# An attention and Fourier kernel: eight banks and later loads in the Projection, Fourier tiles split later, and another order in the prologue's last block

## The chip, the cores and the metric

The kernel runs on one NeuronCore of a Trainium2 chip. The metric is device microseconds from one launch, smaller is better. The core has five engines that work side by side, each through its own instructions in order: TensorE (PE, matmuls; its weight loads are shown as PEld), VectorE (DVE), ScalarE (ACT), GpSimd (POOL) and SyncE (SP), which here gives out most of the DMA transfers. GpSimd gives out some too. TensorE writes only to PSUM, which has eight banks; VectorE and ScalarE empty them.

## The reference

Two layers of attention, each followed by a Fourier mixing layer, on one sequence of 2048 tokens with 640 features and 32 heads of 20:

```python
def _A_ref(x, wqkv, wo):
    ...
    q, k, v = qkv[0], qkv[1], qkv[2]
    scores = jnp.einsum("bhqd,bhkd->bhqk", q, k) * (Dh ** -0.5)
    p = _softmax(scores, axis=-1)
    o = jnp.einsum("bhqk,bhkd->bhqd", p, v)
    return (lambda x, *d: x.transpose(*d))(o, 0, 2, 1, 3).reshape(B, S, D) @ wo

def _B_ref(x, dft_seq_re, dft_seq_im, dft_hid_re, dft_hid_im):
    a = jnp.einsum("bsd,ed->bse", x, dft_hid_re)
    b = jnp.einsum("bsd,ed->bse", x, dft_hid_im)
    y = jnp.einsum("ts,bse->bte", dft_seq_re, a) - jnp.einsum("ts,bse->bte", dft_seq_im, b)
    return y

x = A_x
x = x + _A_ref(_layernorm(x, axis=-1), A_wqkv, A_wo)
x = x + _B_ref(_layernorm(x, axis=-1), ...)
x = x + _A_ref(_layernorm(x, axis=-1), A_wqkv, A_wo)
x = x + _B_ref(_layernorm(x, axis=-1), ...)
```

## The kernel before

**Arithmetic.** Operands are split into a high and a low part (`split`, L85: one copy that rounds, one subtraction), and most products are made of three matmuls, high by high, high by low and low by high (`three`, L93, and `passes`, L100). One layer runs through four stages.

**Prologue** (`Qkv.prologue`, L293). The rows are normalized and transposed in four blocks of 512 tokens. For each block `tb` a product of 15 matmuls (L103) is made for the first chunk of q (k = 0 in the loop) and one for the first chunk of k (k = 1). `keep` (L198) empties each: ScalarE writes the rounded part and the squares (L218), for k VectorE takes the maximum of the squares over the blocks (L220), VectorE writes the low part (L221), and GpSimd gives out the store of both (L222). `norms` (L225) sums the squares over the features of a head with one matmul (L230) and takes their maximum (L231). Then come the values of four token tiles (`own`, L336), 15 matmuls each, which ScalarE empties (L263). Behind the last block's norms the code writes out, in this order: `bound` (L456), which makes from the norms' maxima the shift that goes into the exponent and stores it (L465); `qshift` (L519), four loads of shift rows into the q tiles (L522), for which the store must have landed; and `kload` (L492), eight loads of the second half of k. These stand ahead of the values of that block in the code; the values need none of them. The attention's first scores need the shift rows.

**Attention** (`Attention.sweep`, L571). 512 steps of scores (L536), exponentials on ScalarE (L539) and value sums (L547), with the remaining products of q, k and v in between. Each finished block of queries is emptied and divided by VectorE (`finish`, L552) and written to the tensor o by GpSimd's DMAs (L568). The last of these belong to the last quarter of the tokens.

**Projection** (`Project.run`, L1087). Eight stages p of two token tiles n = 2p, 2p + 1. `product(n)` (L1013) multiplies the tile of o by wo, in two halves of 15 matmuls, each into a bank of its own; for n up to 4 three of the five feature chunks were done during the attention (`begin`, L998), and 12 matmuls a product remain. VectorE adds the product to the residual rows (L1021). `moments(p)` (L1030) stores the sum (L1033), squares it on ScalarE (L1039), makes mean and scale on GpSimd, and folds mirrored columns on VectorE (L1050, L1051). `normal(k)` (L1070) normalizes and folds the rows of stage k some stages later; four of these folds end in the operands `xn` of the Fourier stage. Three kinds of transfers go through SP's queue in the order of the code: `load(p + 3)` (L1008, L1011) brings residual rows into one of four tiles, the one that stage p - 1 used; `fetch` (L983, L990) brings o for two pairs of stages at a time, in stages 1 and 3, four calls of two transfers each, into the tiles that the products just made have left; and the store of `moments`. In stage 1 three tiles of Fourier coefficients are loaded as well (L1209).

**Fourier** (`Fourier.run`, L1340). 16 sums, each of nine matmuls, go over the coefficient tiles in `ORDER`; `accumulate` (L1224) adds tile m into three banks, b0 to b2 or b3 to b5. After the last tile of four, `turn` (L1237) copies and splits the three banks. `parts(i)` (L1211) splits the raw coefficient tile of position i: one ScalarE copy (L1217), one VectorE subtraction (L1219), into one of six buffers, so that position i takes the buffer of position i - 6. Positions 0 to 5 are split during the Projection, the others in this loop. `middle` (L1242) works out one single row in four steps between the sums; its third step is twelve small matmuls (L1267, pturn) on a row that VectorE has made (L1257, L1259, L1262). `hidden` (L1297) makes the second transform, eight times.

What the code says ahead of the change, in the places that it touches:

```python
p = bank(f"b{4 + (2 * n + i) % 4}", [128, 512], "py")[:, :HD]     # Project.product
...
if p:                                                             # Project.run
    s.load(p + 3)
for n in (2 * p, 2 * p + 1):
    s.product(n)
...
s.parts(i + s.AHEAD)                                              # Fourier.run, AHEAD = 6
```

The order in each queue is that of the code: nothing is reordered between the instructions of one engine.

Of the kernel before, what the change touches and what calls it, by code (L numbers as in the profile page):

```python
# [19 lines left out]
ND = D // 128  # L20
NT = S // 128
NB = S // 512
# [3 lines left out]
NQ = NT // 4  # L26
# [6 lines left out]
HD = D // 2  # L33
# [6 lines left out]
def mha_fnet_kernel(ctx, tc, x_in, wqk, wv, wo, seq, hid, nat_seq, nat_hid, out):  # L40
# [33 lines left out]
    def bank(tag, shape, name):  # L74
        return pools["pool"].tile(list(shape), F32, name=name, tag=tag)
# [60 lines left out]
    class Qkv:  # L136
# [58 lines left out]
        def product(s, p, w, tb, dc):  # L195
            return passes(p, (w[:, 0, dc], w[:, 1, dc]), s.xt[tb, dc], dc)
# [96 lines left out]
        def prologue(s, vals, xt, fill, att):  # L293
            s.xtp, s.fill, room = xt, fill, s.room
            if s.given:
                for k in (2, 3):
                    s.load(k)
            s.top = const.tile([128, 2, ND, NB], F32, name="top", bufs=2)
            V.memset(s.top, 0.0)

            def values():
                s.wv = fill("wv", [ND, 2, HD], F32R, "wv")
                for dc in range(ND):
                    split(s.wv[:, dc, 0], s.wv[:, dc, 1], s.wvraw[dc])

            if s.given:
                s.turn(0)
                values()
            else:
                s.stats(0)  # L310

                s.fetch(0, att.kq, "k3", wait=True)
                s.fetch(ND, att.kq, "k4")
                for k in (2, 3):
                    s.load(k)
                s.load_values()
                s.norm(0)
                s.stats(1)
                s.early(0)
                s.norm(1)  # L320
                s.early(1)
                s.turn(0, wait=True)
                values()

            def ones(t):
                s.v[t] = vals(f"v{t}", [H * VW + 12], F32, "v")
                G.memset(s.v[t][:, :H * VW].rearrange("p (a c) -> p a c", c=VW)[:, :, DH:], 1.0)
                G.memset(s.v[t][:, H * VW:], 1.0)

            for t in range(NT - ND):  # L330
                ones(t)
            def later(tb, k, f):
                if tb + 2 < NB:
                    f(2 * tb + 4 + k)

            def own(tb, n):  # L336
                t = 4 * tb + n
                p = s.bank([128, HD], "pv")
                for dc in range(ND):
                    for f in s.value(p, t, dc):  # L340
                        f()
                s.own(p, t, 0, False)

            for tb in range(NB):

                sq, late = [], tb == 0
                if late:
                    for k in range(2):
                        later(tb, k, s.load)
                for k in range(2):  # L350
                    p = s.bank([128, 512], "pqk")
                    for dc in range(ND):
                        for f in s.product(p, s.w[k], tb, dc):
                            f()
                    sq.append(s.keep(p, k * ND, tb, False, (room, fill)[k]))
                    if late:
                        s.stats(2 + k)
                        continue
                    later(tb, k, s.stats)
                if late:  # L360
                    for n in range(4):
                        own(tb, n)
                        if n < 2:
                            s.norm(2 + n)
                            later(tb, n, s.stats)
                if tb == 0:
                    att.setup()
                elif tb == 1:
                    for t in range(NT - ND, NT):
                        ones(t)  # L370
                if tb + 1 < NB:
                    s.turn(tb + 1)
                    for k in range(2):
                        later(tb + 1, k, s.load)
                for k in range(2):
                    later(tb, k, s.norm)
                    s.norms(s.bank, k * ND, tb, sq[k])
                if tb == 0:
                    att.qload(0, 0, None)
                elif tb == 1:  # L380
                    s.fetch(ND + 1)
                    for j in range(2):
                        att.kload(0, 0, j)
                elif tb == 2:
                    s.w1 = s.weights(s.fill("w", [2, ND, 128], F32R, "wqk"), ND + 1, True)
                    s.fetch(1)
                    att.zeros(room)
                elif tb == NB - 1:
                    list(s.bound(0, room))
                    att.qshift(0, 0)  # L390
                    for j in range(2):
                        att.kload(0, 1, j)
                if not late:
                    for n in range(4):
                        own(tb, n)
            s.made |= {0, ND}


# [559 lines left out]
    class Project:  # L958
# [54 lines left out]
        def product(s, n):  # L1013
            x = s.x[n // 2][:, n % 2]
            for i in range(2):
                p = bank(f"b{4 + (2 * n + i) % 4}", [128, 512], "py")[:, :HD]
                cols = slice(i * HD, (i + 1) * HD)
                first = DONE if n in s.begun else 0
                for dc in range(first, ND):
                    three(p, *s.operands(n, dc, cols), dc == first, dc == ND - 1)  # L1020
                V.scalar_tensor_tensor(x[:, cols], p, 1.0, x[:, cols], op0=OP.mult, op1=OP.add,  # L1021
                                       accum_out=s.sums(n // 2)[:, i, n % 2:n % 2 + 1])
# [64 lines left out]
        def run(s):  # L1087
            s.ot[2] += s.heads(s.room, 2, (1,))
            s.ot.append(s.heads(s.room, 3))
            for m, part in ((0, 1), (1, 0), (1, 1)):  # L1090
                s.fetch(1, m, part)
            for p in range(NP):
                if p:
                    s.load(p + 3)
                for n in (2 * p, 2 * p + 1):
                    s.product(n)
                if p in (1, 3):
                    for m in range(2):
                        for part in range(2):
                            s.fetch(p // 2 + 2, m, part)  # L1100

                for k in LAG.get(p, [p - 1]):
                    s.normal(k)
                if p in AHEAD:
                    for i in AHEAD[p]:
                        s.next.parts(i, (0,))
                for k in SCALED.get(p, []):
                    s.scale(k)
                s.moments(p)
                if p == 1:  # L1110
                    for _ in range(3):
                        s.next.load(_)
                if p == 3:
                    s.next.edge_sum(0)
                if p in AHEAD:
                    for i in AHEAD[p]:
                        s.next.parts(i, (1,))
                if p == 6:
                    s.next.edge_sum(1)
                    s.next.mids()  # L1120
            for k in (NP - 2, NP - 1):
                s.normal(k)
# [7 lines left out]
    class Fourier:  # L1130
# [209 lines left out]
        def run(s, after):  # L1340
# [6 lines left out]
            for i, m in enumerate(s.ORDER):  # L1347
                tb, ri, q = m // 8, (m // 4) % 2, m % 4
                s.accumulate(m)
                if q == NQ - 1:  # L1350
                    s.turn(tb, ri)
                s.parts(i + s.AHEAD)
                if m in (6, 7, 9, 10):
                    s.middle((6, 7, 9, 10).index(m))
                if 11 <= m < 14:
                    s.hidden(m - 11)
                if m == 13:
                    s.hidden(3)
                    for t in (6, 7):
                        s.residual(t)  # L1360
                if m in (12, 13) and s.dst is not out:
                    k = m - 12
                    s.next[k] = moments([s.x[2 * k + i][:, 0] for i in range(2)], 2, "a")

                if 4 <= i < 10:
                    s.residual(i - 4)
                elif i == 10 and s.dst is not out:

                    s.wraw = [r(tag, [ND, 128], F32, "wraw") for r, tag in ((s.own, "wraw"), (s.late, "raw1"))]
                    for k in range(2):  # L1370
                        nc.sync.dma_start(s.wraw[k], wqk[k * ND])
# [259 lines left out]
```

## Time and profile before

| what | value |
|---|---|
| median of 3 runs | 2456.39 us |
| lowest, highest | 2454.7, 2457.36 us |
| the profiled execution's own time | 2458.13 us |
| its span, from the first to the last instruction | 2456.3 us |
| its mean granted TensorE clock | 0.998 |
| exponentials (L539), 2048 of them | 1918.1 us of ScalarE |
| value sums (L547), 8192 matmuls | 1030.0 us of TensorE |
| scores (L536), 4096 matmuls | 746.6 us of TensorE |

In the first layer the prologue ends at 86 us, the attention at 1101, the Projection at 1163; in the second layer the attention begins at 1305, the Projection at 2320 and the Fourier stage at 2380. A row of the timeline has start and duration in us, the engine, the line of the kernel, the operation, what is written from what, and a count; in square brackets stand the idle time before it and the instruction that ended it. Durations of matmuls are modelled and overlap, so the step from one start to the next is the better measure. "SPq" marks a transfer that SP gives out; its duration is the giving out, not the transfer. A row of a list of waits has the waiting group, what released it, the total, the count and the longest.

### The profile page before, as it was taken

The numbers are of one execution on the slowest core, as the hardware profiler recorded it, in microseconds if no ns is written. First come the engines' busy times: TensorE is split into PE (matmuls) and PEld (weight loads), VectorE is DVE, ScalarE is ACT, GpSimd is POOL, SyncE is SP. The second block draws the span as 40 slices with busy tenths as digits, with TensorE's granted clock in tenths as the row PEclk, the third lists the DMA queues.
The fourth block names the chain that finished last, engine by engine and source line by source line (L and its number), as shares of the span: only waits on it lengthen the run. The fifth ranks groups of instructions, "written<-read, shape, count | busy, mean of one in ns | idle before, by whom it ended". The sixth has DMA issues, their size and how long they took to land. (4 is left out here: it accounts for less than half of the span.)

```text
span 2456.3 us, 43826 instructions
## 1 busy us (share of the span) xinstructions
PE 2425.9 (99%) x16320; PEld 1169.0 (48%) x16320; DVE 995.6 (41%) x2246; ACT 2116.0 (86%) x2428; POOL 529.0 (22%) x1032
## 2 busy tenths in 40 slices
PE   8999999999999999999999999999999999999998
PEld 7644444443333333349795444444433333333596
DVE  6244442234343333427762434323423332333275
ACT  6699998899999999985457999888999999999862
POOL 2012211112112212114321212211112211222143
PEclk9999999999999999999999999999999999999999
DMA  5224231223232325318452332312221322253175
GB/s 184 101 89 126 82 112 53 78 67 116 73 92 88 95 80 171 95 47 278 175 201 95 107 107 85 118 53 70 77 83 57 92 64 68 58 152 83 61 248 198
DMA packets 128226, 262.63 MB, mean 107 GB/s; under 512 B 29936, under 2 KB 54288, under 8 KB 128004
## 3 DMA queue, kind: packets, MB, share of 16 engines
q1 hardware_dynamic: 89412, 159.89, 20.3%
q0 software_dynamic: 38592, 99.85, 12.8%
q8 instruction: 131, 2.15, 0.4%
q14 instruction: 91, 0.75, 0.1%
HBM read 175.29 MB, written 84.31 MB: 106 GB/s over the span
## 5 line engine op out<-in xcount | busy, mean ns | idle before, releaser
L539 ACT ACTIVATE e<-psc 128x1024 f32<-128x1024 f32 x2048 | 1918.1, 1059 | 107.9 <-PE psc L536 97.6
L547 PE MATMUL acc<-e,v 128*32 128x512 f32 x8192 | 1030.0, 600 | 0.4 <-DVE of L554 0.3
L536 PE MATMUL psc<-stq,stk 62*128 62x512 f32 x4096 | 746.6, 445 | 1.9 <-ACT e L539 0.5
L536 PEld LDWEIGHTS psc<-stq,stk 62*128 62x128 f32 x4096 | 334.4, 184 | 705.5 <-ACT e L539 565.0
L547 PEld LDWEIGHTS acc<-e,v 128*32 128x32 f32 x8192 | 211.0, 108 | 406.5 <-issue 368.6
L103 PE MATMUL pqk<-xt,wqk 128*128 128x512 f32 x1200 | 319.2, 407 | 0.0
L568 POOL DMA_DIRECT2D o<-oh x256 | 131.1, 521 | 826.2 <-DVE oh L563 814.4
L88 DVE CAST hl<-pqk 128x512 fp32r<-128x512 f32 x64 | 44.3, 692 | 605.6 <-PE pqk L103 605.6
L103 PEld LDWEIGHTS pqk<-xt,wqk 128*128 128x128 f32 x1200 | 213.3, 188 | 82.8 <-issue 39.4
L103 PE MATMUL pv<-wv,xt 128*128 128x320 f32 x960 | 151.2, 313 | 0.0
L103 PEld LDWEIGHTS pv<-wv,xt 128*128 128x128 f32 x960 | 141.0, 188 | 15.5 <-issue 11.7
L554 DVE STREAM_TRANSPOSE of<-acc 128x512 f32<-128x512 f32 x64 | 45.8, 715 | 225.8 <-PE acc L547 225.8
L568 POOL DMA_DIRECT2D o<-ot x256 | 128.2, 508 | 1.9 <-issue 0.9
L222 POOL DMA_DIRECT2D scrq<-hl x40 | 28.3, 706 | 426.0 <-DVE hl L91 239.5
L222 POOL DMA_DIRECT2D scrk<-hl x40 | 27.7, 694 | 393.0 <-DVE hl L91 253.2
L96 PE MATMUL py<-wo,o 128*128 128x320 f32 x320 | 101.3, 317 | 2.8 <-DMA o<-o 1.5
L98 PE MATMUL py<-wo,o 128*128 128x320 f32 x320 | 99.1, 310 | 2.2 <-DMA o<-o 2.2
L817 DVE TENSOR_REDUCE far<-cq 128x1 f32<-128x512 f32 (+5 forms) x169 | 98.5, 584 | 5.7
L97 PE MATMUL py<-wo,o 128*128 128x320 f32 x320 | 98.7, 308 | 0.0
L821 DVE TENSOR_TENSOR cq<-cq 128x512 f32<-128x512 f32 (+4 forms) x166 | 96.4, 581 | 4.0 <-DMA cq<-in_nat_seq_dram 3.3
L261 DVE COPY v<-pv 128x320 f32<-128x320 f32 x32 | 15.7, 490 | 161.3 <-PE pv L103 161.3
L96 PEld LDWEIGHTS py<-wo,o 128*128 128x128 f32 x320 | 60.0, 188 | 10.2 <-issue 5.8
(204 smaller groups left out, 1736.0 us busy)
## 6 DMA issues: line engine op xcount, KB each, us to landing
cq<-in_nat_seq_dram POOLq DMA_DIRECT2D x64, 512.0 KB, 5.3
scrq<-hl POOLq DMA_DIRECT2D x40, 512.0 KB, 3.2
scrk<-hl POOLq DMA_DIRECT2D x40, 512.0 KB, 3.1
stq<-scrq SPq DMA_DIRECT2D x256, 80.0 KB
stk<-scrk SPq DMA_DIRECT2D x128, 160.0 KB
o<-o SPq DMA_DIRECT2D x32, 384.0 KB
stq<-scrq SPq DMA_DIRECT2D x256, 40.0 KB
stk<-scrk SPq DMA_DIRECT2D x128, 80.0 KB
```

The costliest lines, as they stand in the source:

```text
L96: PE.matmul(out_ap, ah, bh, start=start, stop=False)
L97: PE.matmul(out_ap, ah, bl, start=False, stop=False)
L98: PE.matmul(out_ap, al, bh, start=False, stop=stop)
L103: yield lambda i=i, j=j, k=k: PE.matmul(out_ap, a[i], b[j], start=dc == 0 and k == 0, stop=dc == ND - 1 and k == 2)
L222: G.dma_start(s.scr["qk"[k]][c * 128:(c + 1) * 128, :, tb * 512:(tb + 1) * 512], hl.bitcast(F32))
L536: PE.matmul(p[:, i], s.k[g, kc // 8, j][r, kc % 8 * 128:(kc % 8 + 1) * 128], s.q[g, qb, j][r], start=True, stop=True)
L539: A.activation(e, p, AF.Exp, scale=SCALE)
L547: PE.matmul(s.acc[32 * j:32 * j + 32], s.a.v[kc][:, v0:v0 + 32], s.e[n, j // 2][:, j % 2], start=kc == 0, stop=kc == NT - 1, skip_group_ch ...
L554: V.transpose(t0.rearrange("p b c -> p (b c)"), s.acc)
L568: G.dma_start(s.o[k, h * DH:(h + 1) * DH, qb * 512:(qb + 1) * 512], hl[k][32 * j:32 * j + DH])
L817: V.tensor_reduce(to, x, op=OP.max, axis=AX.X, apply_absolute_value=True)
L821: V.tensor_tensor(y, x, y, op=op)
```

## The change

Four edits in three places. In the prologue's last block the product of k comes ahead of that of q; k's norm follows the two products, and q's norm with the bound, the shift rows and the loads of k is called from within the values of the first token tile, after two of five feature chunks (six matmuls). In the Projection the products go round all eight banks, beginning with b4, instead of round b4 to b7, and `load(p + 3)` comes behind `moments(p)` instead of ahead of the products. In the Fourier loop position 10 is split at i = 6 instead of i = 4, and so on to position 15 at i = 11 instead of 9; positions 6 to 9 stay where they are.

```diff
-            def own(tb, n):
+            def own(tb, n, between=None):
...
                 for dc in range(ND):
                     for f in s.value(p, t, dc):
                         f()
+                    if between and dc == 1:
+                        between()
                 s.own(p, t, 0, False)
...
-                sq, late = [], tb == 0
+                sq, late, last = {}, tb == 0, tb == NB - 1
...
-                for k in range(2):
+                for k in (1, 0) if last else (0, 1):
                     p = s.bank([128, 512], "pqk")
...
-                    sq.append(s.keep(p, k * ND, tb, False, (room, fill)[k]))
+                    sq[k] = s.keep(p, k * ND, tb, False, (room, fill)[k])
...
-                for k in range(2):
+                for k in range(1 if last else 0, 2):
                     later(tb, k, s.norm)
                     s.norms(s.bank, k * ND, tb, sq[k])
...
-                elif tb == NB - 1:
+
+                def bounds():
+                    s.norms(s.bank, 0, tb, sq[0])
                     list(s.bound(0, room))
                     att.qshift(0, 0)
                     for j in range(2):
                         att.kload(0, 1, j)
+
                 if not late:
                     for n in range(4):
-                        own(tb, n)
+                        own(tb, n, bounds if last and n == 0 else None)
...
-                p = bank(f"b{4 + (2 * n + i) % 4}", [128, 512], "py")[:, :HD]
+                p = bank(f"b{(4 + 2 * n + i) % 8}", [128, 512], "py")[:, :HD]
...
             for p in range(NP):
-                if p:
-                    s.load(p + 3)
                 for n in (2 * p, 2 * p + 1):
                     s.product(n)
...
                 s.moments(p)
+                if p:
+                    s.load(p + 3)
                 if p == 1:
                     for _ in range(3):
                         s.next.load(_)
...
-                s.parts(i + s.AHEAD)
+                if i < 4:
+                    s.parts(i + s.AHEAD)
+                elif i >= NQ + 2:
+                    s.parts(i + s.AHEAD - 2)
```

## The prediction

> **What bounds the kernel now.** I read the page first, then the waits of TensorE alone, then the timeline of four short stretches, then the waits of SP's queue.
>
> ```profile
> span 2456.3 us, 43826 instructions
> PE 2425.9 (99%) x16320; PEld 1169.0 (48%) x16320; DVE 995.6 (41%) x2246; ACT 2116.0 (86%) x2428; POOL 529.0 (22%) x1032
> ```
>
> The span and the first engine row: TensorE (PE) is busy in 99% of the span, so whatever stands in its way is scarce. The list of TensorE's own waits is short; three of its rows are here, and those for tiles of o are seen as rows of the timeline in part 2.
>
> ```profile
> PE pn L230 <- DVE sq L220: 1.8, 2, 0.9
> PE py L96 <- DVE xr L1021: 1.4, 2, 0.7
> PE pturn L1267 <- DVE c3raw L1259: 0.9, 1, 0.9
> ```
>
> The columns are the waiting group, its releaser, the total, the number of waits and the longest. There is one wait per layer in the prologue (pn), one per layer in the Projection for a PSUM bank (py on xr), and one in the first Fourier stage (pturn). All lie where the change works. What they cost is read from starts of matmuls, since the durations shown overlap.
>
> **Part 1: the prologue's last block.**
>
> ```profile
> 75.83 0.39 PE L230 MATMUL pn<-sq,ind 128*32 128x512 bf16 x1
> 77.09 0.38 PE L230 MATMUL pn<-sq,ind 128*32 128x512 bf16 x1 [0.88 <-DVE sq L220]
> 77.40 9.06 PE L103 MATMUL pv<-wv,xt 128*128 128x320 f32 x60
> ...
> 82.22 1.11 SPq L522 DMA_DIRECT2D stq<-shiftb  x4
> ...
> 86.39 1.40 PE L536 MATMUL psc<-stq,stk 62*128 62x512 f32 x6
> ```
>
> Timeline of the first layer: start, duration, instruction, count. The two norm matmuls of q and k start 1.26 us apart, because the second waits for VectorE's maximum of k's squares (L220). From the second to the first value matmul it is 0.31 us, which I take as the price of a norm matmul behind which nothing is late. The change sends k's product first, so its squares and their maximum are made while TensorE computes q's product; q needs no maximum, and its norm comes six value matmuls later. Both norm matmuls stay, the wait goes: 1.26 - 0.31 = 0.95 us a layer, and two layers give **1.90 us**. The exponentials then start as much sooner, for scores follow directly behind the values.
>
> Moved too are the whole of the bounds and their DMAs: q's maximum, the bound, one store of it, four loads of shift rows (L522) and eight loads of k. VectorE still has to take q's low half first, behind the same second product, so I let this chain end when it does today. SP gives out the last shift row at 82.22 + 1.11 = 83.33. The first score would start at 86.39 - 0.95 = 85.44 and needs it, so the chain has 2.1 us for landing where it had 3.06. Today no wait shows there; the landing itself has no row. From above it is bounded by those 3.06 us, and the nearest row below is SP's wait for the store of the same bounds, issued just before:
>
> ```profile
> SPq L522 <- DMA shiftb<-sh: 1.2, 1, 1.2
> ```
>
> With 1.2 us the scores lose nothing, with 3.06 all 0.95 us a layer. A load of as few bytes is nearer to that store, so I take 0.
>
> [...] No run shown here has that landing by itself.
>
> **Part 2: eight banks in the Projection.** Each product of 30 matmuls takes two banks; of four, the third product (n=2) must wait until VectorE has added the first.
>
> ```profile
> 1104.41 0.31 PE L98 MATMUL py<-wo,o 128*128 128x320 f32 x1
> 1105.40 0.42 PE L96 MATMUL py<-wo,o 128*128 128x320 f32 x1 [0.68 <-DVE xr L1021]
> ...
> 1141.44 0.31 PE L98 MATMUL py<-wo,o 128*128 128x320 f32 x1
> 1143.21 0.38 PE L96 MATMUL py<-wo,o 128*128 128x320 f32 x1 [1.46 <-DMA o<-o]
> ...
> 1144.24 0.41 PE L98 MATMUL py<-wo,o 128*128 128x320 f32 x1 [0.51 <-DMA o<-o]
> 1144.50 0.31 PE L96 MATMUL py<-wo,o 128*128 128x320 f32 x1
> ...
> 1145.53 0.30 PE L97 MATMUL py<-wo,o 128*128 128x320 f32 x1
> 1146.54 0.42 PE L98 MATMUL py<-wo,o 128*128 128x320 f32 x1 [0.71 <-DMA o<-o]
> ...
> 2360.77 0.30 PE L97 MATMUL py<-wo,o 128*128 128x320 f32 x1
> 2362.06 0.42 PE L98 MATMUL py<-wo,o 128*128 128x320 f32 x1 [0.99 <-DMA o<-o]
> ```
>
> From 1144.50 to 1145.53 there are seven undisturbed steps, 0.147 us each. The bank costs 1105.40 - 1104.41 - 0.147 = 0.84 us, and the two waits of this kind (1.4 us in all, longest 0.7) say that it is the same in both layers: **1.68 us**. With eight banks n=2 goes to b0 and b1, which the attention's scores left long before, and n=4 is the first to reuse one.
>
> The price is at the far end. Products 14 and 15 now lie in b0 to b3, where the first Fourier sums begin, and these were free.
>
> ```profile
> 1160.63 0.49 DVE L1021 SCALAR_TENSOR_TENSOR xr<-py,xr 128x320 f32<-128x320 f32 x1 [0.58 <-PE py L98]
> 1162.63 0.40 PE L96 MATMUL pacc<-chl,xn 128*128 128x512 f32 x1
> ```
>
> VectorE adds the half of product 15 in b2 at 1160.63, and the sums start 2.0 us later and come to b2 only with their third tile. VectorE waited for TensorE here, so it follows if TensorE is sooner. I take 0; if VectorE stayed where it is, product 15's half would be ready at 1160.63 + 0.49 = 1161.12, and with all of parts 2 and 3 gained (4.06 us in this layer) it would be wanted six matmuls after 1158.57, at 1159.45 or later: at most 1.7 us.
>
> **Part 3: loads behind stores.** Now the SP queue of the same stretch.
>
> ```profile
> 1114.37 0.38 SPq L1011 DMA_DIRECT2D xr<-in_x_dram  x1
> 1114.80 4.84 SPq L990 DMA_DIRECT2D o<-o  x8
> 1119.81 0.88 SPq L1033 DMA_DIRECT2D d_x<-xr  x1
> ...
> 1129.08 0.38 SPq L1011 DMA_DIRECT2D xr<-in_x_dram  x1
> ...
> 1137.46 0.37 SPq L1011 DMA_DIRECT2D xr<-in_x_dram  x1
> 1137.92 5.14 SPq L990 DMA_DIRECT2D o<-o  x8
> ```
>
> ```profile
> SPq L1011 <- DMA d_x<-xr: 26.2, 4, 7.6
> ```
>
> L1011 loads residual rows into a tile whose previous contents are still being stored (L1033). SP waits 26.2 us in four such places, and everything behind it in the queue waits too: at 1137.46 the eight fetches of o for products 12 to 15 (L990), although their tiles were free when product 7 ended, just before VectorE stopped waiting for it:
>
> ```profile
> 1124.19 0.49 DVE L1021 SCALAR_TENSOR_TENSOR xr<-py,xr 128x320 f32<-128x320 f32 x1 [1.13 <-PE py L98]
> ```
>
> They are given out until 1143.06, and product 12 starts at 1141.59 and finds nothing. This is the DMA wait above: 1.62 us at 1143.21, 0.74 at 1144.24 (two steps off), 0.86 at 1146.54, together 3.22 us; in the second layer 1.14 us at 2362.06.
>
> The change puts each such load behind the stage's fetches and its store. Then the first eight fetches (today 1114.80) no longer stand behind the load, but their second half reads what the last attention block writes:
>
> ```profile
> o<-ot POOLq DMA_DIRECT2D x4, 40.0 KB, 5.9
> ```
>
> That lands 5.9 us after its issue in this stretch, so I let them end no sooner than about 1117, then store, load and three Fourier loads until about 1121. The next load waits for that store; the longest landing seen is that of the store at 1119.81, which held SP to 1129.08, 9.3 us. So the second eight fetches start at about 1127 at the latest and land, at the 5 us that today's took from first issue to TensorE's restart, by 1137. Product 12 will ask at 1141.59 - 0.84 = 1140.75. The wait goes whole: 3.22 + 1.14 = **4.36 us**. Each load still has its use three stages on: the one moved from 1114.37 to about 1119 is wanted by the addition at 1132.
>
> **Part 4: Fourier tiles split two sums later.** The first Fourier stage loses time where the second does not.
>
> ```profile
> 1181.68 1.16 ACT L1217 ACTIVATE chl<-craw 128x512 fp32r<-128x512 f32 x2 [4.56 <-DMA craw<-in_seq_dram]
> 1182.74 1.54 ACT L90 ACTIVATE u<-pacc 128x512 fp32r<-128x512 f32 x3
> ...
> 1183.84 0.31 PE L98 MATMUL pmid<-xn,mids 128*66 128x320 f32 x1
> ...
> 1197.20 0.40 PE L96 MATMUL pacc<-chl,xn 128*128 128x512 f32 x1
> ...
> 2400.87 0.31 PE L98 MATMUL pmid<-xn,mids 128*66 128x320 f32 x1
> ...
> 2411.73 0.40 PE L96 MATMUL pacc<-chl,xn 128*128 128x512 f32 x1
> ```
>
> ScalarE stood at 1181.68 before tiles 10 and 11, whose data had not landed (4.56 us, by the row), and only then emptied the finished sums (L90). VectorE came late after it, to the small matmuls (pturn, 0.9 us of wait). After the change the copies of the sums are ahead of tile 10. Between the same two matmuls lie 13.36 us in the first layer and 10.86 in the second, where the data came in time: **2.50 us** to gain, in the first layer only. The tiles themselves are wanted four sums after they are split instead of six. Four sums are 36 matmuls, at least 36 x 0.147 = 5.3 us, and a split takes ScalarE 0.58 us (1.16 for two, above), so I set nothing against it.
>
> ```profile
> 1192.00:1196.00 4.00, 4.00 (x16) 0.64 0.53 200
> ```
>
> (Stretch, its length, TensorE's busy time, granted clock, share and rate of the DMAs.) Part of the 2.50 us is the clock: it was 0.64 in these 4 us, 1.44 us lost, directly behind the wait. [...]
>
> **The sum.** 1.90 + 1.68 + 4.36 + 2.50 = 10.44 us. The profiled execution took 2458.13 us, its span 2456.3 and 1.8 around it: 2447.69. It lies 1.74 us above the median of the three runs and above the highest of them, and if the slow clock (1.44 us) is in that execution alone, the median has 9.0 to gain: 2456.39 - 9.0 = 2447.39. I forecast **2447.5**, and 2444.6 to 2450 as the range of this case by itself: at its lower end every run has the slow clock (2456.39 - 10.44 = 2445.95), less half the spread of the three runs (1.33).
>
> **The rivals.**
> *The fetches stay late.* The store's landing, not the order, may set SP's pace: if it takes over 13 us, product 12 waits as today. For it: 9.3 us and bandwidth shared with fetches that now come sooner. Against it: the four us between 1137 and 1140.75. 4.36 us come back: 2451.9.
> *The attention keeps the prologue's gain.* Scores may wait for the shift rows. For it: the chain of bounds does not move. Against it: 2.1 us for a few KB. 1.90 come back: 2449.4.
> *The new order of splits does nothing or was no cause.* If the small matmuls wait for VectorE anyway, 2.50 come back: 2450.0. Against it speaks the second layer.
> *Slower: the residual rows come late.* Moved behind eight fetches and a store, a load given out near 1119 must land before the addition of its rows.
>
> ```profile
> 1132.13 0.48 DVE L1021 SCALAR_TENSOR_TENSOR xr<-py,xr 128x320 f32<-128x320 f32 x1
> ```
>
> That leaves 13 us. Past it VectorE, which works in order, drags stage after stage, and TensorE stands once eight banks are full, so each further us costs one in each layer: 2447.5 + 2 x (landing - 13). It decides from a landing of 17.5 us on, where the time is that of today; at 20 us it is 2461.5. Against it: the load's own predecessor, the store, needed 9.3 us in the worst place.
>
> **How the numbers follow.** Forecast 0.57; late fetches 0.14; attention keeps it 0.12; splits without effect 0.10; late rows 0.07. A difference under 0.2%, 4.9 us, cannot be told from none, so faster begins at 2451.5. Forecast, attention and splits lie on that side, 0.79, less 0.03 for two of them together; late fetches and that 0.03 are "same": 0.17; slower 0.07. The range reaches from 2444.6 to 2453.0, past the late fetches; outside lies most of the late rows.
>
> **What would show it.** In the changed profile the norm matmuls have no wait on L220 and scores start near 85.4; no py waits for xr L1021 at the third product; fetches of o are given out before 1128 and no py waits for o; the stretch of 13.36 us in the first Fourier stage is near 10.9 at full clock. I am wrong if py still waits for o, if psc's first matmul waits for DMA, if sums wait for L1021 in b0 to b3, or if the additions (L1021) wait for residual rows.

## The result, and the profile after

| what | before | after |
|---|---|---|
| median | 2454.9 us (7 runs) | 2447.74 us (7 runs) |
| lowest, highest | 2454.22, 2457.36 us | 2447.52, 2448.03 us |
| profiled execution, its span | 2458.13, 2456.3 us | 2448.03, 2446.2 us |

The ratio is 0.9968, 95% interval 0.9956 to 0.998: the change takes off 7.2 us, 0.32%, and the runs now lie within 0.5 us of each other. The four further runs of before lowered its median from 2456.39; its profiled execution is slower than all seven, so the two profiles differ by more (10.1 us of span) than the medians.

The page of after, its span and first engine row, and then TensorE's own waits, its complete list (waiting group, releaser, total, count, longest):

```profile
span 2446.2 us, 43822 instructions
PE 2423.5 (99%) x16320; PEld 1168.3 (48%) x16320; DVE 995.9 (41%) x2246; ACT 2115.4 (86%) x2428; POOL 528.8 (22%) x1032
```

```profile
PE ptr L167 <- ACT xa L130: 8.7, 2, 8.4
PE psc L541 <- ACT e L544: 0.5, 2, 0.2
PE acc L552 <- DVE of L559: 0.4, 2, 0.2
```

The waits for the maximum of k's squares (pn), for the third product's bank and for o (py) and for the single row (pturn) are gone. In the timeline of after the prologue's last block reads (lines below the edits have moved by 5):

```profile
76.01 0.39 PE L230 MATMUL pn<-sq,ind 128*32 128x512 bf16 x1
76.33 1.14 PE L103 MATMUL pv<-wv,xt 128*128 128x320 f32 x6
77.40 0.39 PE L230 MATMUL pn<-sq,ind 128*32 128x512 bf16 x1
77.72 8.18 PE L103 MATMUL pv<-wv,xt 128*128 128x320 f32 x54
...
82.33 1.11 SPq L527 DMA_DIRECT2D stq<-shiftb  x4
...
85.83 1.40 PE L541 MATMUL psc<-stq,stk 62*128 62x512 f32 x6
```

From the first norm matmul to the scores it was 75.83 to 86.39, 10.56 us; now it is 9.82, so 0.74 us less, and as much in the second layer. The lone norm inside the values costs 0.51 us and not 0.31: from 76.33 to 77.40 six value matmuls take 1.07 us, 0.19 more than six steps of 0.147. SP's queue in the Projection, and TensorE and VectorE at its end:

```profile
1107.11 6.92 SPq L995 DMA_DIRECT2D o<-o  x8
1114.12 0.42 SPq L1038 DMA_DIRECT2D d_x<-xr  x1
1114.97 0.38 SPq L1016 DMA_DIRECT2D xr<-in_x_dram  x1
...
1122.21 0.38 SPq L1016 DMA_DIRECT2D xr<-in_x_dram  x1
1122.68 9.23 SPq L995 DMA_DIRECT2D o<-o  x8
```

```profile
SPq L1016 <- DMA d_x<-xr: 13.8, 4, 5.0
```

```profile
1158.06 0.40 PE L96 MATMUL pacc<-chl,xn 128*128 128x512 f32 x1
...
1159.45 0.39 PE L96 MATMUL pacc<-chl,xn 128*65 128x512 f32 x1
```

```profile
1156.06 0.49 DVE L1026 SCALAR_TENSOR_TENSOR xr<-py,xr 128x320 f32<-128x320 f32 x1 [0.54 <-PE py L98]
```

The second eight fetches of o start at 1122.68 instead of 1137.92. SP's wait for stores is 13.8 us over both layers, by the row above; in the first layer's Projection alone it is 7.3 us instead of 26.2. The sums start at 1158.06 instead of 1162.63, come to b2 with their third tile at 1159.45, and VectorE, which waits for nothing but TensorE there, has emptied it at 1156.06 + 0.49 = 1156.55. Last, ScalarE and TensorE in the first Fourier stage, and the window in which the clock could have fallen:

```profile
1176.01 1.56 ACT L90 ACTIVATE u<-pacc 128x512 fp32r<-128x512 f32 x3 [3.47 <-PE pacc L1239]
1177.46 0.63 ACT L1222 ACTIVATE chl<-craw 128x512 fp32r<-128x512 f32 x1
```

```profile
1179.27 0.31 PE L98 MATMUL pmid<-xn,mids 128*66 128x320 f32 x1
...
1190.11 0.40 PE L96 MATMUL pacc<-chl,xn 128*128 128x512 f32 x1
```

```profile
1187.00:1191.00 4.00, 3.86 (x24) 3.28 (x23) 1.07 (x3) 1.12 (x3) 0.00 (x0) 1.00 0.66 251
```

The finished sums are copied first and tile 10 comes after them without a wait; between the two matmuls that were 13.36 us apart lie 10.84, at full clock. Lengths of TensorE's stages, from the start of one's first matmul to that of the next (the scores, the first product, the first Fourier sum, the second transform):

```
us                    before     after
attention, layer 1    1014.55    1014.90
Projection, layer 1     61.69      57.33
Fourier, layer 1        36.69      34.17
second transform to scores of layer 2   106.03   105.33
attention, layer 2    1014.53    1014.79
Projection, layer 2     59.78      57.30
Fourier, layer 2        34.18      34.17
```

With 0.56 us less ahead of the first scores (86.39 and 85.83) these make 10.0 of the 10.1 us. The attention, which no edit touches, became 0.6 us longer; the experiments explain that only in part.

### The profile page after: what moved, and what is told of

Read it like the earlier page. It is cut to its first block, busy times and chain, and to the rows that moved or that the text cites. A ratio compares the mean times of both kernels' runs of the same rounds, so it can differ in the third digit from the quotient of the medians.

```text
span 2446.2 us, 43822 instructions
## 1 busy us (share of the span) xinstructions
PE 2423.5 (99%) x16320; PEld 1168.3 (48%) x16320; DVE 995.9 (41%) x2246; ACT 2115.4 (86%) x2428; POOL 528.8 (22%) x1032
## 3 DMA queue, kind: packets, MB, share of 16 engines
q8 instruction: 131, 2.15, 0.4%
## 5 line engine op out<-in xcount | busy, mean ns | idle before, releaser
L231 DVE TENSOR_REDUCE top<-pn 32x1 f32<-32x512 f32 x50 | 33.7, 676 | 76.7 <-PE pn L230 76.5
```

## The experiments

Each is set against the kernel before as it was timed at the same time; its medians there were 2455.32 us (33 runs) for the first four, 2455.0 (32) for the next four and 2455.5 (22) for the last four. First each part alone, in the kernel before.

**Eight banks alone** (`banks_only`).

```diff
-p = bank(f"b{4 + (2 * n + i) % 4}", [128, 512], "py")[:, :HD]
+p = bank(f"b{(4 + 2 * n + i) % 8}", [128, 512], "py")[:, :HD]
```

> Only the eight banks of the Projection are put into the kernel before. My theory: the waits are in series. The third product no longer waits 0.84 us for VectorE, but product 12 still waits for the same fetches of o, whose start SP's queue sets and not TensorE, so TensorE only waits 0.84 us longer there. The Projection stays at 61.7 us (first product matmul to first Fourier sum) in the first layer and 59.8 in the second, within 0.4, and the time is within 0.1% of before. Rival: the parts add as in the prediction; 60.85 and 58.94 us, and 1.7 us less in all.

Measured: 2454.48 us (2452.01 to 2457.52), ratio 0.9997 (0.9988 to 1.0006), 0.84 us below before's median: between the two expectations and not to be told from zero. Its profiled execution had a Projection of 57.62 and 59.04 us, in both layers shorter than the theory had it. Its SP queue in the first layer and its TensorE waits, which are both of the second layer, at product 12:

```profile
1134.71 4.94 SPq L990 DMA_DIRECT2D o<-o  x8
```

```profile
PE py L96 <- DVE xr L1021: 0.6, 1, 0.6
PE py L98 <- DMA o<-o: 0.5, 1, 0.5
```

The second eight fetches were given out 3.2 us earlier than in the profile of before, and of the 3.2 us of waiting for o in the first layer nothing is left in the list, although the edit moves the products by 0.8 us only. So a profile of this kernel with its loads first shows one draw of a wait that varies: in the six such profiles of this study the first layer's Projection took 57.62, 58.24, 59.50, 59.67, 61.69 and 63.28 us.

**Loads behind stores alone** (`loads_only`).

```diff
 for p in range(NP):
-    if p:
-        s.load(p + 3)
...
     s.moments(p)
+    if p:
+        s.load(p + 3)
```

> Only the residual loads of the Projection go behind the stores. My theory: no wait for o is left, the wait of the third product for its bank stays at 0.7 us in each layer, and the Projection takes the 57.3 us of the changed kernel and 0.84, so 58.2 us in both layers; 5.1 us less in all. Rival: sooner by three us in the middle of the stage, TensorE runs into VectorE with four banks, further waits for xr L1021 appear, and the stage takes 59 us or more.

Measured: 2452.1 us (2450.61 to 2454.11), ratio 0.9989 (0.998 to 0.9998). The Projection took 58.24 us in both layers, as expected, with no wait for o. The median fell by 3.2 us, less than 5.1, presumably because the profile of before waited longer for o than its median run; no run shows that.

**Later Fourier splits alone** (`fourier_only`).

```diff
-s.parts(i + s.AHEAD)
+if i < 4:
+    s.parts(i + s.AHEAD)
+elif i >= NQ + 2:
+    s.parts(i + s.AHEAD - 2)
```

> Only the Fourier tiles are split two sums later. My theory: the wait of the twelve small matmuls goes and with it the slow clock behind it; from the first sum to the first matmul of the second transform it is 34.2 us in both layers (36.7 and 34.2 before). In the profile 2.5 us are gained; in the median less, since I take the slow clock to fall only in some executions of the kernel before, those near 2456.5 and not those near 2454.7: 0.9 to 2.5 us, and the spread of the runs shrinks to under 1 us. [...]

Measured: 2453.38 us (2451.42 to 2455.57), ratio 0.9991 (0.9982 to 1.0), 1.9 us less; both Fourier stages 34.18 us. The spread stayed at 4 us, so that part of the expectation is wrong: the waits for o are still in its profile, and are the likely cause:

```profile
PE py L98 <- DMA o<-o: 2.9, 3, 1.1
```

**The prologue's order alone** (`prologue_only`).

```diff
-for k in range(2):                          # products
+for k in (1, 0) if last else (0, 1):
...
-for k in range(2):                          # norms
+for k in range(1 if last else 0, 2):
...
+def bounds():                               # q's norm, bound, qshift, kload,
+    s.norms(s.bank, 0, tb, sq[0])           # called inside the values
```

> Only the order in the prologue's last block is changed. My theory: from the norm of k to the first score it is 9.8 us in the first layer (as in the changed kernel) where the two norms and the values took 10.6, so 0.75 us a layer; the attention passes it on whole, and 1.5 us are gained. Rival: the attention takes 0.3 us longer in each layer, as the profile of the changed kernel shows it, because its loads do not move with its start; then 0.9 us are gained in all.

Measured: 2457.77 us (2454.49 to 2460.76), ratio 1.001 (1.0001 to 1.0019): 2.4 us **slower**. The prologue did what it should (9.82 us from norm to scores), but the second layer's attention took 1017.54 us, 3 us more. ScalarE's waits for scores in the middle of that attention, first for the kernel before and then for this one, and two places of this one's timeline:

```profile
ACT e L539 <- PE psc L536: 48.1, 107, 0.9
```

```profile
ACT e L544 <- PE psc L541: 51.9, 108, 1.1
PE psc L541 <- ACT e L544: 1.5, 5, 0.3
```

```profile
1354.67 5.61 ACT L544 ACTIVATE e<-psc 128x1024 f32<-128x1024 f32 x6 [1.04 <-PE psc L541]
1371.30 5.61 ACT L544 ACTIVATE e<-psc 128x1024 f32<-128x1024 f32 x6 [0.76 <-PE psc L541]
...
1421.56 3.77 ACT L544 ACTIVATE e<-psc 128x1024 f32<-128x1024 f32 x4 [1.03 <-PE psc L541]
```

Once in about 67 us ScalarE starts 1.04 us after it went idle and not 0.76. Set against `fourier_only`, whose attention is not slow, these are steps of 0.25 to 0.4 us, twelve in all; the attention's code is the same. The second set takes one part out of the kernel after.

**After without the prologue's order** (`no_prologue`): its hunk reversed.

> The kernel after, with the prologue's last block as it was before; banks, later loads and later Fourier splits stay. Theory: the reordered prologue gives 0.56 and 0.70 us in its two layers and the attention gives back 0.35 and 0.26 us, as the two profiles show, so without it the time is the after kernel's 2447.7 plus about 0.65: 2448.0 to 2449.3, the steps from the last norm to the scores are again 10.56 and 9.30 us, and the runs stay within about 1 us of each other. Rival: the reordered prologue costs, as it did alone (+2.45 us in the median there, with an attention of 1017.5 us in the second layer), and the gain is all of the other three: then the time is 2445.2 to 2446.5, below the kernel after.

Measured: 2448.99 us (2448.55 to 2449.18), ratio 0.9975 (0.9965 to 0.9984): 1.25 us above after, as the theory had it; the steps are 10.56 and 9.31 us, the attentions 1014.67 and 1014.56.

**After with the loads first** (`after_loads_first`): `load(p + 3)` again ahead of the products.

> The kernel after, with the residual loads ahead of the products again, as before. Theory: the loads' order is what takes the waits for o away; with the old order SP stands before a store's landing and the second eight fetches of o start after 1130 us, so the waits for o come back, different from run to run: the median 2 to 4.5 us above 2447.7 (2449.7 to 2452.2), the runs over 2 us apart, the Projection between 57.3 and 62 us. Rival: the eight banks alone start the products so differently that the store lands in time: then within 1 us of 2447.7, and no wait for o.

Measured: 2452.59 us (2450.31 to 2456.22), ratio 0.9991 (0.9982 to 1.0): 4.85 us above after, a little more than expected, and a spread of 6 us. The Projection was 63.28 and 58.74 us in the profile, the first beyond the 62 that were expected, with the waits for o back:

```profile
PE py L96 <- DMA o<-o: 2.6, 2, 2.4
PE py L98 <- DMA o<-o: 0.8, 2, 0.5
```

```profile
1144.00:1148.00 4.00, 4.00 (x15) 4.00 (x16) 3.96 (x7) 3.43 (x7) 3.21 (x5) 0.50 1.07 333
```

The first layer lost 5.9 us, more than twice its 2.7 us of waits in the list. Directly behind the longest of them, 2.4 us, the granted clock was 0.50 for the whole of this window, and its matmuls stand 0.267 us apart instead of 0.147; over 18 such steps that makes 2.2 us. So the price of a late fetch can have the slow clock in it too.

**After with four banks** (`after_four_banks`): `b{4 + (2 * n + i) % 4}` again.

> The kernel after, with the products round four banks again. Theory: the wait for the third product's bank is a cost in series with nothing else late, 0.84 us in each layer: Projection 58.1 to 58.3 us in both layers, 2449.4 us with runs within 1 us. Rival: the wait is hidden, because the fetches of o decide afterwards (alone, the eight banks gave only 0.84 us in the median): then within 0.5 us of 2447.7.

Measured: 2449.26 us (2448.71 to 2450.14), ratio 0.9976 (0.9967 to 0.9985), 1.5 us above after. The Projection took 58.24 us in both, 0.9 us more in each layer, with one wait of this kind in each and none for o. Here the bank is worth about its whole wait. Alone its median fell by half of that, which cannot be told from zero; that TensorE then spends ahead of a late transfer what it gained is the likely reason, and no run isolates it.

**After with early Fourier tiles** (`after_tiles_early`): `s.parts(i + s.AHEAD)` again.

> The kernel after, with the Fourier tiles split where they were before. Theory: ScalarE again stands before coefficient tiles 10 and 11, the small matmuls wait about 0.9 us for VectorE, and the first layer's stage is 35.8 to 36.7 us instead of 34.17: 2449.3 to 2450.3, where the upper end has the slow TensorE clock. Rival: with loads later in SP's queue the coefficient tiles come at other times, the wait is gone, and the time is within 0.5 us of 2447.7; or they come later still, and the stage is over 37 us.

Measured: 2452.93 us (2449.61 to 2454.31), ratio 0.9989 (0.998 to 0.9998): 5.2 us above after, twice what was expected at most. The Fourier stage, 36.83 us, accounts for 2.66, with the rows that the theory named (ScalarE's timeline, TensorE's waits and a window with its clock):

```profile
1177.36 1.15 ACT L1222 ACTIVATE chl<-craw 128x512 fp32r<-128x512 f32 x2 [4.71 <-DMA craw<-in_seq_dram]
```

```profile
PE pturn L1272 <- DVE c3raw L1264: 0.9, 1, 0.9
```

```profile
1186.00:1190.00 4.00, 4.00 (x17) 2.90 (x17) 1.67 (x8) 1.02 (x6) 0.00 (x0) 0.70 0.83 315
```

The rest, 2.53 us, is again in the second attention, 1017.32 us, step for step as in the prologue's order alone. TensorE also waited 0.3 us for o in this profile, for fetches given out ahead of the stages, which the loads' order does not touch.

In the runs so far the prologue's order with early Fourier splits has the slow attention, with the other two edits or without them; with late splits it has not. No edit of these stands in the attention. What an edit elsewhere can change is the length of ScalarE's stream of instructions ahead of it, as semaphore instructions come or go. Counting ScalarE's records in each trace from 0, semaphore instructions included, up to the first exponential of each layer, gives:

```
                      first exponential is record   attention, us
                         layer 1   layer 2          layer 1   layer 2
before                      97      2401            1014.55   1014.53
banks_only                  97      2401            1014.52   1014.65
loads_only                  97      2401            1014.51   1014.56
fourier_only                97      2399            1014.64   1014.60
no_prologue                 97      2399            1014.67   1014.56
after                       95      2395            1014.90   1014.79
after_loads_first           95      2395            1014.85   1014.89
after_four_banks            95      2395            1014.89   1014.88
prologue_only               95      2397            1014.66   1017.54
after_tiles_early           95      2397            1014.63   1017.32
prologue_two_act            97      2399            1014.74   1015.00
after_two_act               97      2397            1014.62   1017.23
norms_together              95      2395            1014.79   1014.71
norms_and_five_act          97      2401            1014.61   1014.45
```

Set against `fourier_only`, each of the twelve exponentials that come late in `prologue_only` is a record whose number leaves 63 when divided by 128: 2495, 2623, 2751, 2879, 3263 and so on to 4159. In the kernel before the records 2495 to 3263 of this row are late too, by 0.25 to 0.3 us, but it is another exponential that stands there, two places earlier in the pattern, and two or three exponentials on, where ScalarE waits for scores anyway, the time is made up; from 3391 to 4031 nothing shows. At 2397 the record is the exponential behind such a wait, and it is not made up. The last four rows belong to the runs that follow, which test this.

The smaller differences do not follow the position alone: at record 95 the first attention took 1014.63 and 1014.66 us in two kernels and 1014.79 to 1014.90 in four.

**Two idle copies on ScalarE, in the prologue's order alone** (`prologue_two_act`) **and in after** (`after_two_act`), both in the first layer's prologue:

```diff
+pad = room("pad", [1], F32, "pad")
+for _ in range(2):
+    A.activation(pad, zero, AF.Copy)
```

> The reordered prologue alone, as in the run prologue_only, with two copies of one column on ScalarE added in the first layer's prologue; nothing reads them. Theory: ScalarE loses about 0.28 us at every 128th instruction of its stream, and what that costs hangs on which exponential stands there. The first exponential of the second layer was ScalarE's record 2397 in both kernels whose second attention took 1017.3 to 1017.5 us, and 2395, 2399 or 2401 in all others. With two more instructions it is 2399: the second attention takes 1014.6 us again, no steps at intervals of two query blocks, and the median falls from 2457.8 to 2453.8 to 2455.0. Rival: the lost 3 us come from the moved shift rows and k loads or from the Fourier stage's timing before them; then two idle copies change nothing: attention 1017.5, median 2457.8.

> The kernel after with the same two idle copies on ScalarE in the first layer's prologue. Theory: the first exponential of the second layer moves from record 2395 to 2397, the position of the slow attention: it takes 1017.2 to 1017.6 us instead of 1014.8, in steps of about 0.28 us and 0.39 us; the first layer's exponentials move from 95 to 97, the position of the kernel before, and its attention falls from 1014.9 to 1014.55. Together 2449.7 to 2450.6 us. Rival: position in the stream does not matter: within 0.3 us of 2447.7, with both attentions as after.

Measured: the prologue's order alone takes 2454.39 us (2452.43 to 2456.51), ratio 0.9997 (0.9988 to 1.0006), 3.4 us less than without the copies; after takes 2450.28 us (2449.73 to 2451.58), ratio 0.9981 (0.9972 to 0.999), 2.5 us more. Two instructions that compute nothing removed the slow attention from the one kernel (1015.00 us, though not the 1014.6 expected) and put it into the other (1017.23), with steps at the same twelve records. ScalarE's waits for scores, in the same window as above, for the first and then the second:

```profile
ACT e L547 <- PE psc L544: 48.3, 102, 0.8
```

```profile
ACT e L547 <- PE psc L544: 51.0, 107, 1.0
PE psc L544 <- ACT e L547: 1.5, 5, 0.3
```

The rival falls. The first layer of after went from 1014.90 to 1014.62, as expected too; the rows at record 95 above show that this is no proof.

**Both norms together** (`norms_together`).

```diff
-for k in range(1 if last else 0, 2):
+for k in range(2):
     later(tb, k, s.norm)
-    s.norms(s.bank, k * ND, tb, sq[k])
+    if not last:
+        s.norms(s.bank, k * ND, tb, sq[k])
...
 def bounds():
-    s.norms(s.bank, 0, tb, sq[0])
+    for k in (1, 0):
+        s.norms(s.bank, k * ND, tb, sq[k])
```

> The kernel after with k's norm moved too, to directly ahead of q's norm, six value matmuls into the first token tile. Theory: the step that one norm matmul adds inside the values is 0.5 us when it stands alone (0.31 for itself and 0.19 more), and 0.3 when the other stands beside it, so the way from the last product to the scores is 0.2 us shorter in each layer: 2447.2 to 2447.5. Rival: nothing to gain, or the shift rows come later, as the bound waits for both norms: 2447.7 or up to 0.5 us above.

Measured: 2446.97 us (2446.56 to 2447.21), ratio 0.9966 (0.9954 to 0.9979), 0.8 us below after. The timeline of its prologue:

```profile
75.64 1.04 PE L103 MATMUL pv<-wv,xt 128*128 128x320 f32 x6
76.61 0.60 PE L230 MATMUL pn<-sq,ind 128*32 128x512 bf16 x2
77.15 8.19 PE L103 MATMUL pv<-wv,xt 128*128 128x320 f32 x54
85.27 1.40 PE L543 MATMUL psc<-stq,stk 62*128 62x512 f32 x6
```

From the first matmul behind the products to the scores it is 9.63 us, where after has 9.82 (76.01 to 85.83): 0.19 us less in each layer, as expected. That matmul also follows the product's last one after 0.23 us here and after 0.32 in after, where it is a norm: 0.09 more, so 0.28 a layer. With the attentions, 0.11 and 0.08 us shorter, this makes 0.75 of the 0.8 us.

**The same with five idle copies** (`norms_and_five_act`), two in the first layer's prologue and three in the second's.

> As norms_together, with two idle copies in the first layer's prologue and three in the second's, so that ScalarE's first exponentials stand at records 97 and 2401, where the kernel before had them. Theory: the attentions take 1014.55 us each instead of 1014.90 and 1014.79, 0.6 us less than norms_together: 2446.5 to 2447.0. Rival: the 0.3 us per attention are the prologue's gain that the attention gives back, whatever the position: as norms_together, 2447.2 to 2447.7.

Measured: 2446.49 us (2446.33 to 2446.79), ratio 0.9965 (0.9952 to 0.9979), attentions of 1014.61 and 1014.45 us. It beats both kernels, by 1.25 us the changed one. Of the 0.6 us that were expected over `norms_together` 0.48 came. The rival falls: the attention gives nothing back here, with the prologue's order in place.

## Why the prediction was right, and where its steps were off

The forecast was 2447.5 and the time is 2447.74. The mechanisms were those that it named, and the four signs came, except that the scores start at 85.83 and not near 85.4. That the number is so close is luck in part. For the profiled execution the terms were right in sum, 10.44 forecast against 10.1, because what the prologue gave too little, 1.2 us with the attention counted, the Projection largely made up, 6.84 for 6.04. From there the forecast took 9.0 us off 2456.39; the medians differ by 7.2 only, but the 2456.39 of three runs was 1.5 us high, and these two errors cancelled.

What each part is worth by the medians, alone (before less it) and taken out of after:

```
us                predicted   alone    out of after
prologue's order     1.90     -2.45      1.25
eight banks          1.68      0.84      1.52
later loads          4.36      3.22      4.85
Fourier splits       2.50      1.94      5.19
```

Alone they make 3.55 us. With the slow attention out of the prologue's row (`prologue_two_act` against its own before, 2455.5 - 2454.39 = 1.11) they make 7.1, about the gain of all together; but by the intervals of the ratios each is uncertain by some 2 us, so this does not show that the parts add. In the last column 2.53 of the 5.19 are the slow attention, and the loads' row presumably holds what the banks lose when the loads are first, and the slow clock behind the wait.

**Part 1**: the wait went and the shift rows were not late, so the chain of bounds and its DMAs cost nothing. The term was over-sized: 0.95 us a layer forecast, 0.74 measured in both, because a norm among value matmuls costs 0.51 us and not 0.31. From the bounds of the landing nothing more can be said than that 85.83 - 83.44 = 2.4 us were enough; it has no row of its own. Beyond it the forecast had no term for the attention, which became 0.35 and 0.26 us longer. The rival, "the attention keeps the prologue's gain", named a cause that isn't there (late shift rows); of the 0.6 us that were given back a shift of ScalarE's stream regained some 0.4 (`norms_and_five_act`), and why the first layer's part came stays open.

**Part 2**: the mechanism as forecast, 0.9 us a layer for 0.84. The far end, priced at 0 with up to 1.7, cost 0: VectorE moved forward with TensorE, and b2 was empty 2.9 us before it was wanted.

**Part 3**: the wait went whole in both layers, and the second fetches started 4 us ahead of the bound that I gave; giving them out took 9.2 us and not the 5 that I carried over, and still ended at 1131.9, well ahead of 1140.75. Against the 58.2 us of `after_four_banks`, which has the bank waits alone, the profile of before had lost 3.5 and 1.5 us, so 5.0 for 4.36. What I had not seen is that this wait differs from run to run by several us (57.62 to 63.28 us of Projection in the six profiles), and that the clock can fall behind it (0.50 in `after_loads_first`). "The fetches stay late" fell with the start at 1122.68, "the residual rows come late" with the additions (L1026), which in VectorE's whole list of waits wait for TensorE alone, 10.6 us in twelve places.

**Part 4**: 2.50 forecast, 2.52 in the profiles. The clock's part of it was over-sized. Six profiles have early tiles and the pturn wait of 0.9 us; in three of them the clock fell behind it (0.64 before, 0.70 above, and 0.60 in `prologue_two_act`):

```profile
1188.00:1192.00 4.00, 4.00 (x15) 2.97 (x15) 1.67 (x8) 1.02 (x6) 0.00 (x0) 0.60 0.92 350
```

The stage took 36.7 to 37.0 us in these, 35.8 to 36.4 in the other three (`banks_only`, `loads_only`, `prologue_only`), and 34.16 to 34.18 in all eight with late tiles, which have no such wait. The means of the two groups are 0.7 us apart, where the prediction set 1.44 for the clock; the profiles without a drop have another wait, 0.5 to 1.1 us for VectorE's splits of the sums (u), where those with one have 0 to 0.4. So behind the same wait of 0.9 us the clock fell in three profiles of six, and no run shows what decides that. Nor does one show that the profiled execution of before was alone in having the slow clock, which the forecast's 9.0 us supposes. The rival that the splits do nothing was wrong. Parts 3 and 4 together also go with the spread: kernels with both edits have runs within 0.5 to 1.9 us, those with one of them or none within 3 to 7 us.

## What to carry to other kernels

Before a wait is priced, ask whether it belongs to the program or to the execution: a transfer that queues behind a landing store gave another wait in each of six profiles here (57.62 to 63.28 us for the same stage), and the edit that removed it in the kernel after shows in the spread (0.5 us instead of 6) as well as in the median (4.85 us). What is gained ahead of such a wait may be spent in it (eight banks made 0.84 us alone and 1.52 in after; no run isolates the reason), so it is better to size single parts where it is gone. And where an edit loses time in a stage that it doesn't touch, as the second attention here lost 2.5 to 3 us, compare the position of that stage's instructions in their engine's stream before looking for a cause in the data.

## What the runs showed of the hardware

ScalarE starts 0.25 to 0.4 us late at records of its stream that lie 63 beyond a multiple of 128: at twelve of them in the second attention of each slow kernel, at some of the same in the kernel before. At others, as at 3391 to 4031 of before, nothing shows. Whether the attention then takes 2.5 to 3 us more was decided by a shift of two instructions, 2397 against 2395 or 2399. The page of after has two queues of the kind that it calls instruction:

```profile
q8 instruction: 131, 2.15, 0.4%
q14 instruction: 91, 0.75, 0.1%
```

The packets of the first are 2.15 MB / 131 = 16.4 KB each, those of the second 0.75 MB / 91 = 8.2 KB. In time the second lie close to some of the late records' places: in the trace of `prologue_only` a packet of the second queue starts within 1.5 us of 23 of the 36 ScalarE records that leave 63 when divided by 128, and of none of the 36 that leave 127; in that of after it is 25 of 36 and none of 35. In three kernels here the late starts were not made up: their second attention took 1017.23 to 1017.54 us, that of the others 1014.45 to 1015.00. That the packets are what makes ScalarE late is an inference; shown is that the position decides between the slow attention and the others.
